# A conv-and-mixer kernel on one core: the second chunk's k, the inverse-transform constant and two pieces of w_mod asked for earlier

## The chip, the core and the metric

One core of a Trainium2 chip runs the whole kernel. The metric is device time in microseconds (us). The engines are TensorE (PE; PEld is its weight load), VectorE (DVE), ScalarE (ACT), GpSimd (POOL) and SyncE (SP). Each runs its own instructions strictly in the order in which they were written; this kernel's order is written out by hand, and no scheduler moves it. Loads are asked for by a queue, nearly all of them by SP's, a few at the start by ACT's. They are then carried by 16 shared DMA engines.

## What is computed

The reference takes a sequence of S = 2048 rows and D = 640 columns through two residual blocks, both modulated by a vector `c`:

```python
mod = (_silu(c) @ w_mod)                # 6 rows of 640: sa, ca, ga, sb, cb, gb
h = layernorm(x) * (1 + ca) + sa
k_shift[t] = sum_{s<4} k[t - s] * shift_k[:, s]          # short causal convolution
kv = k_shift * v
y = causal_conv(kv, ssm_k) + kv * ssm_D                  # 2048 taps, by FFT
x = x + ga * (h * y)
h = layernorm(x) * (1 + cb) + sb
x = x + gb * (gelu(h^T @ w1 + b1) @ w2 + b2)^T           # mixing over the 2048 rows
```

Here x is first `A_q`. All is float32.

## The kernel before

The first block runs over five chunks of 128 columns (`c` = 0 to 4). The causal convolution is done as a Fourier transform in two steps, both as matmuls with constants. `step1` (L211) is the first step: side 1 for the long taps `ssm_k`, side 0 for kv. Its four parts each end in an ACT copy to the tile `z` (L221). `f2` (L224) is the second step, in eight groups: 32 matmuls (64 records in the trace) against the constant `w2`, an ACT copy to `kt` (L238), two DVE products into `p` (`mul`, L57) and two POOL sums into `y` (`add`, L57). `i2` (L255) and `i1` (L274) go back; `gate` multiplies with the normalised q and adds to x.

Most elementwise work goes through the helper `TT` at L57, so these instructions are told apart by their tiles.

Before a chunk's transform, `kv_ops` (L172) works out kv in four groups, each with eight instructions: four products with taps, three sums, one product with v. DVE does groups 0, 2 and 3; POOL does group 1. The tile `in` (`T_in`) holds `KX`, the chunk's k, and behind it `VX`, its v. The tile `aux` holds the raw long taps (`KSR`) in its first half and, for the first chunk, kv (`X0`) in its second.

The start of the kernel is one long piece of hand-set order (L441 to L531), then the loop over chunks. What matters here:

- SP asks for chunk 0's k, v and taps, then the shift taps of chunk 1 (`load_taps(1)`, L482), the first half of the constant `w2` (`w2_load(0)`, L492), chunk 1's first k and v, its second k, the second half of `w2`, and its second v. Chunk 1's k goes over chunk 0's in the same tile `in`, so each half waits for DVE and POOL to have read the old one.
- The constant lands in the tile `xa`. ACT spreads it over `w0` and `w1` in eight instructions (`w2_part`, L476). The four of `w0` stand in ACT's order between the four copies of `step1(0, t)`; the four of `w1` stand between the copies of the first four groups of `f2`.
- Next SP asks for q, 32 loads of 160 KB each: rows 8 to 15 ("upper", tile `xb`) with the shift taps of chunk 2 and four small loads of biases and `c` between them (L523 to L528), then rows 0 to 7 (tile `xa`).
- Behind all of q come five pieces of w_mod (`mod_load`, L335; 960 KB each), and between the third and the fourth the constant `c_v1` of the back transform (1 MB). Then the long taps of chunk 1 and the k and v of chunk 2.
- In chunk 0, after `f2`, DVE takes the statistics of q's 16 row groups (L576, L577), then `rstd` (L323). ACT normalises 16 pieces into `aux` (`run(ac)`, L290). PE multiplies each w_mod piece by silu(c) (`mod_part`, L339). Behind the normalisation in ACT's order stands `mod_sum` (L346), which needs all five pieces. `mod_row` (L350) then spreads the result over all partitions, and only behind that in PE's order stands `i1` of chunk 0.

Places where the five pieces land before: two in `aux`, two in `in`, one in `p`.

Of the kernel before, what the change touches and what calls it, by code (L numbers as in the profile page):

```python
# [47 lines left out]
def mixer_kernel(ctx: ExitStack, tc: tile.TileContext, q, k, v, shift_k, ssm_k, ssm_D, w1, b1, w2, b2, c,  # L48
# [36 lines left out]
    KX = T_in[:, 0:2240].rearrange("p (n i) -> p n i", i=64)  # L85
    VX = T_in[:, 2240:4288].rearrange("p (n i) -> p n i", i=64)
    KSP = P.rearrange("p (i m) -> p i m", i=32)
    KSR, X0 = T_aux[:, 0:2048], T_aux[:, 2048:4096]
    A1 = T_aux[:, 2048:4096].rearrange("p (j d) -> p j d", j=16)
    KT = [T_kt[:, 512 * i:512 * i + 512] for i in range(2)]  # L90
    TV = T_kt[:, 1024:1536].rearrange("p (n i) -> p n i", i=64)
# [31 lines left out]
    TAP = tap[:, 512:768].rearrange("p (s i) -> p s i", s=4)  # L123


    def load_k(c, g, engs=(sync, sync), n=1):
        for h in range(2):
            r = slice(64 * h, 64 * h + 64)
            engs[h].dma_start(KX[r, 3 + 8 * g:3 + 8 * (g + n)],
                           dram(k, 8 * g * D + DC * c + 64 * h, [[32 * D, 64], [D, 8 * n], [1, 64]]))  # L130

    def load_v(c, g, engs=(sync, sync), n=1):
# [4 lines left out]

    def load_halo(c):
        for h in range(2):
            sync.dma_start(KX[64 * h + 1:64 * h + 64, 0:3],  # L140
                           dram(k, 29 * D + DC * c + 64 * h, [[32 * D, 63], [D, 3], [1, 64]]))

    def load_taps(c, eng=sync):
# [6 lines left out]

    def load_ks(c, upper=sync):
        for h in range(2):
            (sync, upper)[h].dma_start(KSR[64 * h:64 * h + 64].rearrange("p (i n) -> p i n", i=64),
                           dram(ssm_k, (DC * c + 64 * h) * S, [[32, 64], [S, 64], [1, 32]]))


    def perm_add(c, eng=pool):
        for h in range(2):
            r = KSR[64 * h:64 * h + 1].rearrange("p (i n) -> p i n", i=64)[:, :, 0]
            TT(eng, r, r, DR[64 * h:64 * h + 1], ALU.add)  # L160

    def perm(c):
        for i in (slice(0, 16), slice(16, 32)):
            act.activation(KSP.rearrange("p i (n e) -> p i e n", e=2)[:, i],  # L164
                           KSR.rearrange("p (i e n) -> p i e n", e=2, i=32)[:, i], AF.Copy)


    def taps():

        act.activation(TAP, TR.rearrange("p (i s) -> p s i", s=4), AF.Copy)  # L170

    def kv_ops(g, eng=dve, x=X):  # L172
# [4 lines left out]
        kx = lambda s: KX[:, 8 * g + 3 - s:8 * g + 11 - s, :]  # L177
# [267 lines left out]
    dve.memset(epsc, EPS)  # L445
    for h in range(2):
        dve.memset(KX[64 * h:64 * h + 1, 0:3, :], 0.0)
    both = (sync, act)
    load_taps(0, act)
    load_halo(0)  # L450
# [51 lines left out]
    run(kv_ops(1, pool))  # L502
# [7 lines left out]
    run(kv_ops(0))  # L510
    run(kv_ops(2))

    def load_q(js):

# [5 lines left out]
    pl = [three(t) for t in (T_aux, T_aux[:, 2048:3968], T_in[:, 192:2112], T_in[:, 2112:4032], P)]  # L520

    load_q(range(8, 12))
    load_taps(2)  # L523
    load_q(range(12, 14))
    sync.dma_start(stg[14:30, :], dram(b2, 0, [[128, 16], [1, 128]]))
    sync.dma_start(stg[30:35, :], dram(c, 0, [[128, 5], [1, 128]]))
    sync.dma_start(stg[0:13, :], dram(b1, 0, [[128, 13], [1, 128]]))
    sync.dma_start(stg[13:14, :].rearrange("p (h m) -> p h m", h=2), dram(b1, 1664, [[64, 1], [0, 2], [1, 64]]))  # L528
    load_q(range(14, 16))

    fill = kv_ops(3)  # L531

    def dv(n):
        for _ in range(min(n, len(fill))):
# [3 lines left out]
    for c in range(NC):  # L538
# [3 lines left out]
        for g in range(8):  # L542
            m_, a_ = f2(g)
            if pend_m:
                pend_m()
            if pend_a:
                pend_a()
            pend_a, pend_m = (pend_m and pa_next), m_
            pa_next = a_
            if c:  # L550
                for f_ in ac[2 * g:2 * g + 2]:
                    f_()
            elif g < 3:
                for i in ((0, 1), (2,), (3,))[g]:
                    w2_part(1, i % 2, 32 * (i // 2), 32)
                if g == 2:
                    load_q(range(8))
                    for kk in range(2):
                        mod_load(0, kk, (T_aux[:, 0:1920], T_aux[:, 2048:3968])[kk])
            if cn is None and g < 4:  # L560

                act.activation(X[:, 512 * g:512 * g + 1], epsc, AF.Copy)
                for b in range(2):
                    sync.dma_start(X[64 * b:64 * b + 64, 512 * g:512 * g + 512],
                                   dram(w1, (16 * b + g) * F, [[32 * F, 64], [1, 512]]))
            dv(-(-len(fill) // max((6 if c else 8) - g, 1)))
            if c and cn is not None and g == 3:
                perm_add(cn)
# [12 lines left out]
                load_taps(c + 3)  # L581
        if c == 0:
            for kk in range(2, 5):
                if kk == 3:
                    sync.dma_start(T_v1[:, 0:2048], c_v1)
                mod_load(0, kk, (T_in[:, 192:2112], T_in[:, 2112:4032], P[:, 0:1920])[kk - 2])
# [24 lines left out]
            load_v(2, 2, n=2)  # L611
            mod_sum(tap, T_kt[:, 0:640])
            pool.tensor_scalar(PW, TR.rearrange("p (i s) -> p s i", s=4), 1.0, None, op0=ALU.mult)
# [560 lines left out]
```

## Time and profile before

| | |
|---|---|
| times of three runs | 688.35, 692.94, 1027.85 us (median 692.94) |
| profiled execution: its own time | 682.19 us |
| profiled execution: its span | 680.1 us |
| PE busy | 624.6 us, 92% of the span |
| DVE busy | 499.0 us, 73% |
| ACT busy | 299.9 us, 44% |
| POOL busy | 129.5 us, 19% |
| moved by DMA | 81.23 MB, mean 119 GB/s |
| TensorE clock granted, mean | 0.985 of full |

The change touches the first 105 us of the span, some 15% of it. There DMA moves from 164 to over 400 GB/s. The later part, the mixer, is matmul work that the change leaves alone, so shares over the whole span say little; the prediction reads the first stages by themselves.

How such lines are read: in the timeline each row is the start, the busy time, the engine, the line, the operation, what it writes and reads, and in brackets the idle time of that engine before it with what ended the wait. `SPq` and `ACTq` are the sequencers that issue DMAs. The chain of waits is followed back from the last instruction: its rows are start, length and what the time went to; a DMA in it runs from its issue to its landing. A row by stretches has the stretch and its length, each engine's busy time, the granted clock, the busy share of the DMA engines (packets overlap, so it can pass 1) and the GB/s moved.

### The profile page before, as it was taken

To read this page: it belongs to the slowest core of one execution; us is meant where nothing else is said; L and a number is where in the kernel's file an instruction comes from. 1 tells how busy PE (TensorE), PEld (TensorE's weight loads), DVE (VectorE), ACT (ScalarE), POOL (GpSimd) and SP (SyncE) were. 2 spreads that over 40 slices of the span, in tenths; PEclk is the share of its full clock that TensorE was granted. 3 is DMA by queue.
4 is the path that set the end of the run, shared out by engine and by line. 5 is a ranking of instruction groups with operands and counts; after the bars stand their busy time and mean duration, and the time that the engine had idled before them with its cause. 6 is when DMAs were issued, how large, how long until landed. Compare 5 with 4: busy or idle time off the path is not lost.

```text
span 680.1 us, 20719 instructions
## 1 busy us (share of the span) xinstructions
PE 624.6 (92%) x9113; PEld 592.2 (87%) x9113; DVE 499.0 (73%) x867; ACT 299.9 (44%) x478; POOL 129.5 (19%) x149
## 2 busy tenths in 40 slices
PE   5889578989999999788899999999999989999997
PEld 2888277989989887688899889999999989999997
DVE  6799589979799279888866622321689779888996
ACT  1744645646547365547654222322344133333331
POOL 5562058226035142000000000000000520000000
PEclk9989889999999999999899999999999999999999
DMA  9978998365425343430308333334441634356601
GB/s 185 251 176 245 326 172 177 86 126 131 69 66 180 73 121 115 104 84 1 63 4 151 63 63 63 63 67 112 132 125 56 198 115 124 107 162 167 184 33 39
DMA packets 165522, 81.23 MB, mean 119 GB/s; under 512 B 90774, under 2 KB 157112, under 8 KB 165048
## 3 DMA queue, kind: packets, MB, share of 16 engines
q1 hardware_dynamic: 158516, 78.60, 47.0%
q10 hardware_dynamic: 6916, 1.31, 1.1%
q8 instruction: 71, 1.16, 0.7%
q14 instruction: 19, 0.16, 0.1%
HBM read 69.40 MB, written 10.49 MB: 117 GB/s over the span
## 4 chain that ended last, share of the span: by engine, by line
PE 63%; DVE 19%; DMA 7%; ACT 5%; issue 4%; POOL 1%; SPq 1%; DVEq 0%; ACTq 0%; POOLq 0%
PE pst L437 20%; PE pst L1033 17%; PE pst L1110 7%; PE pst L219 5%; PE pst L263 5%; PE pst L234 4%; DVE p L57 4%; PE pst L283 3%; DMA p<-in_w_mod_dram 2%; DVE tap L57 2%; DVE kt L57 2%; DVE sm L576 1%; PE pst L906 1%; DMA in<-in_A_v_dram 1%; ACT z L272 1%
## 5 line engine op out<-in xcount | busy, mean ns | idle before, releaser
L234 PE MATMUL pst<-z,w 128*64 128x64 f32 x2560 | 79.4, 225 | 13.3 <-DVE p L57 6.5
L234 PEld LDWEIGHTS pst<-z,w 128*64 128x64 f32 x2560 | 77.6, 140 | 15.6 <-issue 7.9
L221 ACT ACTIVATE z<-pst 128x1024 f32<-128x1024 f32 x40 | 42.9, 1073 | 42.1 <-PE pst L219 42.0
L57 POOL TENSOR_TENSOR y<-p 128x256 f32<-128x256 f32 x72 | 51.3, 743 | 41.2 <-DVE p L57 41.1
L57 DVE TENSOR_TENSOR p<-pst,kt 128x512 f32<-128x512 f32 x80 | 50.7, 682 | 6.0 <-ACT kt L238 6.0
L1033 PE MATMUL pst<-r_z,m_w 128*128 128x320 f32 x222 | 42.0, 312 | 2.2 <-DVE m_w L57 2.2
L869 ACT ACTIVATE pst<-pst,sm 128x640 f32<-128x640 f32 x13 | 10.0, 767 | 76.0 <-PE pst L437 76.0
L263 PEld LDWEIGHTS pst<-v,y 32*128 32x128 f32 x1280 | 38.5, 187 | 3.5 <-issue 3.0
L238 ACT ACTIVATE kt<-pst 128x512 f32<-128x512 f32 x40 | 23.9, 597 | 39.8 <-PE pst L234 24.1
L263 PE MATMUL pst<-v,y 32*128 32x64 f32 x1280 | 40.5, 272 | 0.4 <-issue 0.2
L219 PEld LDWEIGHTS pst<-v,p 128*64 128x64 f32 x640 | 34.8, 137 | 6.1 <-ACT p L164 2.9
L1021 ACT ACTIVATE m_w<-m_v 128x896 fp32r<-128x896 f32 x24 | 22.7, 951 | 36.9 <-PE pst L1033 16.8
L219 PE MATMUL pst<-v,p 128*64 128x128 f32 x640 | 36.7, 274 | 2.0 <-ACT p L164 2.0
L1033 PEld LDWEIGHTS pst<-r_z,m_w 128*128 128x128 f32 x222 | 35.2, 190 | 2.4 <-DVE m_w L57 2.4
L57 DVE TENSOR_TENSOR tap<-tap,kt 128x512 f32<-128x512 f32 x51 | 35.5, 697 | 1.3
L57 DVE TENSOR_TENSOR kt<-in,tap 128x512 f32<-128x512 f32 x51 | 35.0, 685 | 1.4
L57 POOL TENSOR_TENSOR m_p<-u_i,r_z 128x320 f32<-128x320 f32 x1 | 0.9, 881 | 183.4 <-issue 183.4
L219 PE MATMUL pst<-v,x 128*64 128x128 f32 x512 | 31.1, 275 | 2.2 <-DVE x L57 1.0
L219 PEld LDWEIGHTS pst<-v,x 128*64 128x64 f32 x512 | 27.9, 137 | 3.2 <-issue 1.6
L272 ACT ACTIVATE z<-pst 128x512 f32<-128x512 f32 x38 | 20.9, 645 | 21.1 <-PE pst L263 21.1
L283 PE MATMUL pst<-z,v 64*64 64x64 f32 x1280 | 23.9, 225 | 6.4 <-issue 3.7
L57 DVE TENSOR_TENSOR m_w<-m_v,m_w 128x896 fp32r<-128x896 f32 x24 | 27.9, 1166 | 2.3 <-ACT m_w L1021 1.8
(296 smaller groups left out, 1486.6 us busy)
## 6 DMA issues: line engine op xcount, KB each, us to landing
x<-in_B_w_dram SPq DMA_DIRECT2D x20, 512.0 KB
aux<-in_A_ssm_k_dram SPq DMA_DIRECT2D x9, 512.0 KB
m_x<-xs SPq DMA_DIRECT2D x28, 160.0 KB
out_dram<-m_x SPq DMA_DIRECT2D x28, 160.0 KB
m_v<-in_B_w_dram SPq DMA_DIRECT2D x9, 448.0 KB
in<-in_w_mod_dram SPq DMA_DIRECT2D x4, 960.0 KB
x<-in_B_w_dram SPq DMA_DIRECT2D x7, 448.0 KB
in<-in_A_v_dram SPq DMA_DIRECT2D x22, 128.0 KB
```

Source lines behind the costliest of these rows:

```text
L57: TT = lambda eng, o, a, b, op: eng.tensor_tensor(o, a, b, op=op)
L219: pe.matmul(ps[64 * ri:64 * ri + 64, o:o + 255:2], lhs, F1[:, 128 * ri:128 * ri + 128], start=True, stop=True)
L221: evac = lambda: act.activation(Z[:, side, t], ps.rearrange("p (a k e) -> p a k e", a=4, e=2), AF.Copy)
L234: pe.matmul(ps[64 * h:64 * h + 64, o:o + 64], W2[k1 // 32][:, 2 * (k1 % 32) + ri], rhs, start=True, stop=True)
L238: act.activation(kt.rearrange("p (m i) -> p m i", i=32), pv[:, :, 1], AF.Copy)
L263: pe.matmul(pp[qd // 2][:, o:o + 64], Y[p, ri, i:i + 2].rearrange("p i k -> p (i k)"), V2[p, 64 * ri:64 * ri + 64], start=ri == 0, stop=ri ...
L272: act.activation(o, i, AF.Copy)
L283: pe.matmul(ps[64 * b:64 * b + 64, 512 * e + 64 * jj:512 * e + 64 * jj + 64], V1[p, ri, n2], T2[p, :, 32 * ri + n2], start=ri == 0, stop=r ...
L437: pe.matmul(ps[0:m, h, 0:320], w_.bitcast(F32R), r_[:, 320 * h:320 * h + 320].bitcast(F32R), start=first and i == 0, stop=last and i == 2)
L1021: act.activation(W[n][0].bitcast(F32R), A[p, w_], AF.Copy)
L1033: pe.matmul(bank[n], w[:, i].bitcast(F32R), r.bitcast(F32R), start=i == 0 and k == 0, stop=i == 6 and k == 2)
L1110: pe.matmul(acc[s][:, h, 0:320], w[:, f_].bitcast(F32R), u[r + h].bitcast(F32R), start=f_ == 0 and k == 0, stop=f_ == NF - 1 and k == 2)
```

## The change

Four things are done together.

1. Chunk 1's k gets a home of its own, `KX1`, in the first 2240 columns of `aux`. For that, the long taps of chunk 0 and its kv (`X0`) move to the tile `y`. All of chunk 1's k (two halo loads and four of 256 KB) is asked for right behind chunk 0's last v, ahead of the shift taps and of `w2`.
2. `c_v1` and the first two pieces of w_mod are asked for between q's upper rows. The five pieces have new homes: `v`, `in`, `aux`, `in`, `p`. The long taps of chunk 1, which go over the third piece, are asked for behind `mod_part` of that piece and no longer behind the first.
3. The shift taps of chunk 2 and the four small loads are issued by POOL's queue, which stand in POOL's order behind chunk 1's kv and ahead of the sums of `f2`. No DMA was issued by POOL before.
4. Three more matmuls (ten for seven) at the start, whose output nobody reads, and two more short memsets for the new home.

```diff
-    KSR, X0 = T_aux[:, 0:2048], T_aux[:, 2048:4096]
+    KSR, X0 = T_aux[:, 0:2048], T_y[:, 0:2048]
+    KX1 = T_aux[:, 0:2240].rearrange("p (n i) -> p n i", i=64)
...
+    kx_of = lambda c: KX1 if c == 1 else KX
+    ksr_of = lambda c: T_y[:, 2048:4096] if c == 0 else KSR
...
+    load_halo(1)
+    load_k(1, 0, n=2)
+    load_k(1, 2, n=2)
     all_taps()
     load_taps(1)
     ps = psum()
-    for _ in range(7):
+    for _ in range(10):
...
     w2_load(0)
-    load_halo(1)
-    load_k(1, 0, n=2)
     load_v(1, 0, n=2)
     run(kv_ops(3, x=X0))
-    load_k(1, 2, n=2)
     w2_load(1)
     load_v(1, 2, n=2)
...
+    homes = [T_v1[:, 2048:3968], T_in[:, 192:2112], T_aux[:, 0:1920], T_in[:, 2240:4160], P[:, 0:1920]]
...
     load_q(range(8, 12))
-    load_taps(2)
+    load_taps(2, pool)
+    for o, t in ((30, dram(c, 0, [[128, 5], [1, 128]])), (14, dram(b2, 0, [[128, 16], [1, 128]])),
+                 (0, dram(b1, 0, [[128, 13], [1, 128]]))):
+        pool.dma_start(stg[o:o + t.shape[0], :], t)
+    pool.dma_start(stg[13:14, :].rearrange("p (h m) -> p h m", h=2), dram(b1, 1664, [[64, 1], [0, 2], [1, 64]]))
+    sync.dma_start(T_v1[:, 0:2048], c_v1)
     load_q(range(12, 14))
...
+    mod_load(0, 0, homes[0])
     load_q(range(14, 16))
-
-    fill = kv_ops(3)
+    mod_load(0, 1, homes[1])
+
+    fill = kv_ops(3, kx_=KX1)
...
             for kk in range(4):
                 mod_part(tap, kk, pl[kk])
-                if kk == 0:
+                if kk == 2:
                     load_D(1)
                     load_ks(1)
```

On SP's queue, from chunk 0's last v to chunk 1's last v, this is the order before (`in` holds k and v, `rows` the shift taps, `xa` the constant `w2`):

```order
L135 DMA in<-in_A_v_dram 64x8x64 x4
L145 DMA rows<-in_A_shift_k_dram 64x256 x2
L473 DMA xa<-in_const_w_dram 128x2048
L140 DMA in<-in_A_k_dram 63x3x64 x2
L129 DMA in<-in_A_k_dram 64x16x64 x2
L135 DMA in<-in_A_v_dram 64x16x64 x2
L129 DMA in<-in_A_k_dram 64x16x64 x2
L473 DMA xa<-in_const_w_dram 128x2048
L135 DMA in<-in_A_v_dram 64x16x64 x2
```

And now:

```order
L139 DMA in<-in_A_v_dram 64x8x64 x4
L144 DMA aux<-in_A_k_dram 63x3x64 x2
L133 DMA aux<-in_A_k_dram 64x16x64 x4
L149 DMA rows<-in_A_shift_k_dram 64x256 x2
L478 DMA xa<-in_const_w_dram 128x2048
L139 DMA in<-in_A_v_dram 64x16x64 x2
L478 DMA xa<-in_const_w_dram 128x2048
L139 DMA in<-in_A_v_dram 64x16x64 x2
```

All of k moved ahead of the shift taps and of both halves of `w2`; what stands ahead of the last v is the same set of loads in both.

Further down SP's queue, from q's upper rows (`xb`) to the last piece of w_mod, before (`g` holds the biases and `c`):

```order
L517 DMA xb<-in_A_q_dram 64x640 x8
L145 DMA rows<-in_A_shift_k_dram 64x256 x2
L517 DMA xb<-in_A_q_dram 64x640 x4
L525 DMA g<-in_B_b_dram 16x128
L526 DMA g<-in_c_dram 5x128
L527 DMA g<-in_B_b_dram 13x128
L528 DMA g<-in_B_b_dram 1x2x64
L517 DMA xb<-in_A_q_dram 64x640 x4
L517 DMA xa<-in_A_q_dram 64x640 x16
L336 DMA aux<-in_w_mod_dram 128x3x640 x2
L336 DMA in<-in_w_mod_dram 128x3x640
L585 DMA v<-in_const_v_dram 128x2048
```

And now:

```order
L522 DMA xb<-in_A_q_dram 64x640 x8
L534 DMA v<-in_const_v_dram 128x2048
L522 DMA xb<-in_A_q_dram 64x640 x4
L340 DMA v<-in_w_mod_dram 128x3x640
L522 DMA xb<-in_A_q_dram 64x640 x4
L340 DMA in<-in_w_mod_dram 128x3x640
L522 DMA xa<-in_A_q_dram 64x640 x16
L340 DMA aux<-in_w_mod_dram 128x3x640
L340 DMA in<-in_w_mod_dram 128x3x640
L340 DMA p<-in_w_mod_dram 128x3x640
```

Three large loads moved from behind q into its upper half, and six small ones left this queue.

They now stand in POOL's order, between the last instruction of chunk 1's kv (`x`) and the sums of `f2` (`y`):

```order
L57 TENSOR_TENSOR x<-t,in 128x8x32x2
L149 DMA rows<-in_A_shift_k_dram 64x256 x2
L532 DMA g<-in_c_dram 5x128
L532 DMA g<-in_B_b_dram 16x128
L532 DMA g<-in_B_b_dram 13x128
L533 DMA g<-in_B_b_dram 1x2x64
L57 TENSOR_TENSOR y<-p 128x8x32 x16
```

Before, the sums stood right behind that instruction.

ACT's order is the same as before. Its part that waits for `w2` reads, in the new kernel (`w_74` is `w0`, `w_75` is `w1`):

```order
L481 ACTIVATE w_74<-xa,v 128x32x32
L225 ACTIVATE z<-pst_262 128x4x128x2
L481 ACTIVATE w_74<-xa,v 128x32x32
L225 ACTIVATE z<-pst_281 128x4x128x2
L481 ACTIVATE w_74<-xa,v 128x32x32
L225 ACTIVATE z<-pst_300 128x4x128x2
L481 ACTIVATE w_74<-xa,v 128x32x32
L225 ACTIVATE z<-pst_319 128x4x128x2
L242 ACTIVATE kt<-pst_378 128x512
L481 ACTIVATE w_75<-xa,v 128x32x32 x2
L242 ACTIVATE kt<-pst_415 128x512
```

Nothing moved here; each copy to `z` and `kt` stands behind a piece of `w2`.

More of the change, by code (lines that the diff above doesn't have):

```diff
@@ L128, in load_k @@
             r = slice(64 * h, 64 * h + 64)
-            engs[h].dma_start(KX[r, 3 + 8 * g:3 + 8 * (g + n)],
+            engs[h].dma_start(kx_of(c)[r, 3 + 8 * g:3 + 8 * (g + n)],
                            dram(k, 8 * g * D + DC * c + 64 * h, [[32 * D, 64], [D, 8 * n], [1, 64]]))
@@ L139, in load_halo @@
         for h in range(2):
-            sync.dma_start(KX[64 * h + 1:64 * h + 64, 0:3],
+            sync.dma_start(kx_of(c)[64 * h + 1:64 * h + 64, 0:3],
                            dram(k, 29 * D + DC * c + 64 * h, [[32 * D, 63], [D, 3], [1, 64]]))
@@ L152, in load_ks @@
         for h in range(2):
[L153 removed]
+            (sync, upper)[h].dma_start(ksr_of(c)[64 * h:64 * h + 64].rearrange("p (i n) -> p i n", i=64),
                            dram(ssm_k, (DC * c + 64 * h) * S, [[32, 64], [S, 64], [1, 32]]))
@@ L158, in perm_add @@
         for h in range(2):
-            r = KSR[64 * h:64 * h + 1].rearrange("p (i n) -> p i n", i=64)[:, :, 0]
+            r = ksr_of(c)[64 * h:64 * h + 1].rearrange("p (i n) -> p i n", i=64)[:, :, 0]
             TT(eng, r, r, DR[64 * h:64 * h + 1], ALU.add)
@@ L164, in perm, with kv_ops @@
             act.activation(KSP.rearrange("p i (n e) -> p i e n", e=2)[:, i],
-                           KSR.rearrange("p (i e n) -> p i e n", e=2, i=32)[:, i], AF.Copy)
+                           ksr_of(c).rearrange("p (i e n) -> p i e n", e=2, i=32)[:, i], AF.Copy)
     def taps():
         act.activation(TAP, TR.rearrange("p (i s) -> p s i", s=4), AF.Copy)
-    def kv_ops(g, eng=dve, x=X):
+    def kv_ops(g, eng=dve, x=X, kx_=KX):
         S_, T_, W_ = (SV, TV, TAP) if eng is dve else (PS_.rearrange("p (n i) -> p n i", i=64),
@@ L176, in kv_ops @@
         w = lambda s: W_[:, None, s, :].to_broadcast([128, 8, 64])
-        kx = lambda s: KX[:, 8 * g + 3 - s:8 * g + 11 - s, :]
+        kx = lambda s: kx_[:, 8 * g + 3 - s:8 * g + 11 - s, :]
         ops = [lambda: TT(eng, S_, kx(3), w(3), ALU.mult)]
@@ L447, in mixer_kernel @@
         dve.memset(KX[64 * h:64 * h + 1, 0:3, :], 0.0)
+        dve.memset(KX1[64 * h:64 * h + 1, 0:3, :], 0.0)
     both = (sync, act)
@@ L501, in mixer_kernel @@
     all_taps()
-    run(kv_ops(1, pool))
+    run(kv_ops(1, pool, kx_=KX1))
     for t in range(4):
@@ L509, in mixer_kernel @@
             w2_part(0, (1, 0, 1)[t], 32 * (t > 0), 32)
-    run(kv_ops(0))
-    run(kv_ops(2))
+    run(kv_ops(0, kx_=KX1))
+    run(kv_ops(2, kx_=KX1))
     def load_q(js):
@@ L519, in mixer_kernel @@
     three = lambda t: [t[:, 640 * j:640 * j + 640] for j in range(3)]
-    pl = [three(t) for t in (T_aux, T_aux[:, 2048:3968], T_in[:, 192:2112], T_in[:, 2112:4032], P)]
+    homes = [T_v1[:, 2048:3968], T_in[:, 192:2112], T_aux[:, 0:1920], T_in[:, 2240:4160], P[:, 0:1920]]
+    pl = [three(t) for t in homes]
     load_q(range(8, 12))
-    load_taps(2)
+    load_taps(2, pool)
[4 more added lines that the diff above has]
+    sync.dma_start(T_v1[:, 0:2048], c_v1)
     load_q(range(12, 14))
[L525 to L528, printed above, removed]
+    mod_load(0, 0, homes[0])
     load_q(range(14, 16))
-    fill = kv_ops(3)
+    mod_load(0, 1, homes[1])
+    fill = kv_ops(3, kx_=KX1)
     def dv(n):
@@ L557, in mixer_kernel @@
                     load_q(range(8))
-                    for kk in range(2):
-                        mod_load(0, kk, (T_aux[:, 0:1920], T_aux[:, 2048:3968])[kk])
             if cn is None and g < 4:
@@ L583, in mixer_kernel @@
             for kk in range(2, 5):
-                if kk == 3:
-                    sync.dma_start(T_v1[:, 0:2048], c_v1)
-                mod_load(0, kk, (T_in[:, 192:2112], T_in[:, 2112:4032], P[:, 0:1920])[kk - 2])
+                mod_load(0, kk, homes[kk])
             step1(0, 0)
```

## The prediction

> **What bounds the kernel now.** I read the chain of waits for the first 105 us first, since the change reaches no further. These are its parts where something other than steady work was waited for:
>
> ```profile
> 0.71 2.61 DMA rows<-in_A_shift_k_dram
> ...
> 20.57 7.03 DMA in<-in_A_k_dram
> ...
> 31.20 8.10 DMA in<-in_A_v_dram
> ...
> 42.60 3.56 PE pst L234 x64
> ...
> 67.05 15.83 DMA p<-in_w_mod_dram
> 82.88 0.04 issue
> 82.92 1.54 PE tap L343 x12
> 84.46 0.02 issue
> 84.48 0.71 ACT kt L347
> ```
>
> Two waits at the start, for chunk 1's k (until 27.59) and its second v (until 39.30), then a long one for the last w_mod piece, until 82.88. Behind it come `mod_sum` at 84.48, the `mod_row`s and `i1`. Next, how busy the DMA engines were while that w_mod piece waited its turn:
>
> ```profile
> 20.00:24.00 4.00, 4.00 (x79) 4.00 (x74) 3.79 (x7) 2.33 (x3) 1.88 (x2) 1.00 0.96 307
> 24.00:32.00 8.00, 7.49 (x134) 7.03 (x130) 5.38 (x8) 7.31 (x8) 4.08 (x4) 1.00 1.19 217
> 42.00:62.00 20.00, 18.44 (x509) 17.98 (x509) 19.49 (x41) 8.24 (x12) 11.39 (x16) 0.91 0.67 194
> 72.00:76.00 4.00, 2.19 (x23) 1.01 (x24) 1.29 (x5) 2.30 (x6) 1.37 (x2) 1.00 1.03 421
> 76.00:80.00 4.00, 0.43 (x6) 0.00 (x0) 2.43 (x2) 4.00 (x11) 0.00 (x0) 1.00 1.03 400
> ```
>
> The last two columns are the share and the GB/s. With `w2` at 20 to 24 us, and with k and v at 24 to 32, the engines are full, at 307 and 217 GB/s. While q is asked for, at 42 to 62, they are at 0.67 and 194 GB/s; with w_mod alone they reach 400 to 421. So between 42 and 62 DMA could have moved some 20 x (410 - 194) = 4.3 MB more: SP, with one 160 KB piece at a time, doesn't ask fast enough. Last the rows of the engines:
>
> ```profile
> 25.28 1.13 ACT L476 ACTIVATE w<-xa,v 128x1024 f32<-128x1024 f32 x1
> 28.77 1.08 ACT L221 ACTIVATE z<-pst 128x1024 f32<-128x1024 f32 x1
> 32.80 1.02 ACT L221 ACTIVATE z<-pst 128x1024 f32<-128x1024 f32 x1
> 33.88 5.82 PE L234 MATMUL pst<-z,w 128*64 128x64 f32 x192 [1.90 <-ACT z L221]
> 36.01 0.60 ACT L238 ACTIVATE kt<-pst 128x512 f32<-128x512 f32 x1 [2.18 <-PE pst L234]
> 36.50 2.18 ACT L476 ACTIVATE w<-xa,v 128x1024 f32<-128x1024 f32 x2
> 38.58 0.59 ACT L238 ACTIVATE kt<-pst 128x512 f32<-128x512 f32 x1
> 39.85 0.69 DVE L57 TENSOR_TENSOR x<-tap,in 128x512 f32<-128x512 f32 x1 [1.14 <-DMA in<-in_A_v_dram]
> 41.18 1.28 DVE L57 TENSOR_TENSOR p<-pst,kt 128x512 f32<-128x512 f32 x2
> 42.97 1.28 DVE L57 TENSOR_TENSOR p<-pst,kt 128x512 f32<-128x512 f32 x2
> 54.41 1.29 DVE L57 TENSOR_TENSOR p<-pst,kt 128x512 f32<-128x512 f32 x2
> ```
>
> `f2` starts at 33.88, but DVE comes to its first product (`mul` of group 0) only at 41.18, behind the kv that waited for v. Its input `kt` was ready at 36.61, so this stage has 4.57 us of slack on ACT and PE. From the second `mul` (42.97) to the eighth (54.41) it is 11.44 us for six groups, 1.9 each. Then DVE takes q's statistics without a break, and this follows:
>
> ```profile
> 68.34 1.97 PE L219 MATMUL pst<-v,x 128*64 128x128 f32 x32
> 70.23 1.28 PE L343 MATMUL tap<-aux,sm 128*32 128x320 f32 x12
> 74.74 3.18 ACT L290 ACTIVATE aux<-xa,sm 128x128 f32<-128x128 f32 x8 [1.69 <-POOL t L613]
> 77.83 3.17 ACT L290 ACTIVATE aux<-xb,sm 128x128 f32<-128x128 f32 x8
> 84.48 0.70 ACT L347 ACTIVATE kt<-tap 96x640 f32<-96x640 f32 x1 [3.48 <-PE tap L343]
> ```
>
> ACT ends the normalisation at 81.00 and idles 3.48 us for w_mod. That is what the second part of the change can win, and no more: with w_mod in time, ACT's own work ends last there.
>
> **The change part by part.**
>
> *w_mod and `c_v1` earlier.* Behind q's last load stood 5 x 0.98 + 1.05 = 5.96 MB, landed at 82.88. Now 3.02 MB of it goes into q's stretch, where 4.3 MB had room; at 410 GB/s that takes 7.4 us off the tail. SP's queue gets no longer: three issues in, six out,
>
> ```profile
> 41.77 1.18 SPq L145 DMA_DIRECT2D rows<-in_A_shift_k_dram  x2
> 63.04 2.08 SPq L336 DMA_DIRECT2D aux<-in_w_mod_dram  x2
> 67.05 1.44 SPq L336 DMA_DIRECT2D p<-in_w_mod_dram  x1
> ```
>
> and the third to fifth piece wait, as before, for chunk 1's kv and the sums from `p`; these end 1.43 behind the eighth `mul`, so by 60 even if that comes late, and SP is then still with q. So the last piece lands at about 82.88 - 7.4 = 75.5. PE is through `step1(0, 3)` at 70.31 and needs five `mod_part`s of 1.3 to 1.5, so 77; ACT is later, at 81.0. `mod_sum` moves from 84.48 to 81.05: **-3.4 us**, if nothing ahead moves. The long taps of chunk 1, now behind `mod_part` 2, go two parts later on PE, at about 74, but onto a queue that is nearly empty; `perm(1)` needs them behind `mod_row`, as before. Nothing.
>
> *k ahead of `w2`.* DMA is full here, so order is all that changes. Before, k's first half landed at 27.59 behind taps, `w2`(0) and halo. Now the same loads and k's second half (0.52 MB, 2.4 us at 217 GB/s) precede the end of `w2`(0): it lands at **30.0**. Before, ACT used it at 25.28 without a wait. For the last v nothing changes, the same bytes stand ahead of it: 39.30 again, and `mul` of group 0 can't start before 41.18. The wait for k on DVE (27.71) turns into one for the shift taps, which now land at about 27.59 + 2.4 less `w2`(0), 1.05 MB or 3.4 us at 307 GB/s, = 26.6; with 0.6 for the taps DVE is ready at 27.3. The v then holds it anyway. Gain there: nothing.
>
> The loss: from 30.0 ACT has four pieces of `w0` and four copies to `z`, with no gaps, 4 x 1.13 + 4 x 1.08 = 8.84, so `f2` starts at 38.9 in place of 33.88. That is 5.0 late against 4.57 of slack. PE meanwhile does three of four `step1` parts; the fourth needs the buffer that the first copy frees at 32.2, and takes 1.97. PE is idle from 34.2 to 38.9. Before, an idle time of 2.91 us on PE was followed by this:
>
> ```profile
> 39.00:42.50 3.50, 0.69 (x24) 0.55 (x20) 2.62 (x5) 1.20 (x2) 0.56 (x1) 0.99 0.68 190
> 42.50:46.00 3.50, 3.40 (x66) 3.42 (x68) 3.50 (x7) 1.63 (x2) 2.77 (x5) 0.52 0.71 200
> ```
>
> The granted clock fell to 0.52, and the group begun at 42.60 took 3.56 us, not 5.82 / 3 = 1.94. I take it that group 0 now runs so: it ends at 42.5, `kt` is there at 43.1, `mul` 0 at 43.2. Then ACT has two pieces of `w1` (2.18) before the next copy (0.59), so `mul` 1 is at 46.0, where it was 42.97: 3.05 late. Six groups at 1.87 (PE's 5.82 / 3 less overlap, and DVE's 1.28 + 0.69 of kv less overlap) end at 57.2 against 54.41: **+2.8 us**. The statistics, `rstd` and the normalisation all follow behind and move by it.
>
> [...]
>
> *Six loads on POOL.* No row shows a DMA issued by POOL. Before, POOL ended kv and began the sums here:
>
> ```profile
> 37.15 1.30 POOL L57 TENSOR_TENSOR x<-t,in 128x512 f32<-128x512 f32 x1
> 41.94 1.43 POOL L57 TENSOR_TENSOR y<-p 128x256 f32<-128x256 f32 x2 [3.49 <-DVE p L57]
> ```
>
> It starts this kv as before (its taps land at 26.6, a product takes 1.3), so it is free at 38.45 again. `mul` 2, now at 47.9, needs the first sums (1.43) done, so POOL has until 46.4: six loads in 8.0 us, 1.33 each, cost nothing. The ends for the unknown price: SP's issue of the same shift taps, 1.18 for two, 0.59 each; and the 2.61 us from issue to landing in the chain's first row, if POOL stayed with each until it landed. I take the low end: an issue doesn't wait for its landing on SP. Nothing, hidden by the wait for `mul` 0.
>
> *The rest.* Three more dummy matmuls delay `step1(1, 0)` by half a microsecond, ahead of ACT's wait for `w2`; nothing. Two memsets on one row, before the first load lands: nothing.
>
> **Sum.** -3.4 + 2.8 = **-0.6 us** against the profiled execution (682.19 us, span 680.1), so 681.6. The runs shown are above it: 688.35 and 692.94, and one of 1027.85 that I leave out; 692.94 is the median. I put the forecast at the middle one of the three that agree, 688.35: 688.35 - 0.6 = **687.7 us**.
>
> **The rivals.**
>
> *PE keeps its clock, or `w2` lands sooner* (faster). With the clock full, group 0 ends at 40.8, `mul` 0 is at 41.5, `mul` 1 at 44.2: 1.2 late, the eighth 1.0, net -2.4. With `w2` in time the whole 3.4 is won. 684.9 to 686. For it: the idle time before was 2.9 us at another point, and the clock row is the only case. Against: DMA was full at 24 to 32, so the bytes must come out somewhere.
>
> *POOL is held by its loads* (slower). At 2.61 each it is free at 38.45 + 15.7 = 54.1, 7.7 behind 46.4; each sum and `mul` behind moves by as much: -0.6 + 7.7 = +7.1, 695.4. It decides from 1.33 us a load upward. For it: nothing on POOL shows a price. Against: SP's 0.59. [...]
>
> *w_mod lands no earlier* (no change). If q and w_mod share what q got alone, the last piece lands at 82.9 again; ACT's end at 81.0 + 2.8 = 83.8 hides behind it, and the sum is zero: 688.35. Against it stand the 400 to 421 GB/s.
>
> **How the numbers follow.** The forecast 0.45, the faster rival 0.25, POOL 0.15, no earlier w_mod 0.15. All four lie within 1.1% of the median, and a measurement of this kernel tells 2% from no change, not less. What could show over 2% is the spread of the runs themselves: from 682.2 to 692.9 is 1.6%. So faster by over 2% 0.06, within 2% 0.89, slower 0.05. The range goes from the lowest level with the faster rival, 682.2 - 3.4 = 678.8, to POOL's 695.4: 679 to 696.
>
> **What would show it.** Right: ACT waits some 4 us for `xa` at 26 to 30; `f2` starts near 38.9; the granted clock falls there; DMA above 300 GB/s from 42 to 62; ACT's `kt` at L347's successor comes right behind the sixteenth normalisation, near 83.9; POOL's loads end before `mul` 0. Wrong: `f2` starting near 34, or w_mod still waited for by PE behind the normalisation, or DVE's products waiting for POOL.

## The result, and the profile after

The changed kernel takes 694.91 us (median of 20 runs, 689.64 to 699.85), the kernel before 688.34 (20 runs): the ratio is 1.0101, with a 95% interval of 1.0074 to 1.0127. It is 1% slower, some 7 us. The forecast was 0.6 us faster. It lies within 2% as forecast, but on the other side, and not by any of the rivals. That 694.91 still falls into the stated range of 679 to 696 is luck: the upper end was POOL's price, which was not paid.

The profiled execution took 694.99 us with a span of 693.2, close to its median; that of the kernel before had been 6 us ahead of its own (682.19). The chain of waits of the changed kernel, its parts from the copy of `w2` to `mod_sum`:

```profile
24.50 5.72 DMA xa<-in_const_w_dram
30.24 1.15 ACT w L481
...
38.28 11.34 PE pst L238 x328
49.62 3.30 issue
52.91 5.21 PE pst L238 x127
58.12 3.93 issue
62.05 2.96 PE pst L238 x57
...
87.74 3.94 ACT aux L294 x10
91.68 0.59 ACT kt L351
```

The reader should see two things. The long wait for w_mod, which stood here before the change (15.83 us, to 82.88), is gone, and `mod_sum` comes right behind ACT's last normalisation. But w_mod is not earlier. The weight load for its fifth piece still waits for the landing, until 85.55, where the forecast had 75.5:

```profile
85.55 0.69 PEld L347 LDWEIGHTS tap<-p,sm 128*32 128x32 f32 x12 [0.63 <-DMA p<-in_w_mod_dram]
```

The wait left the chain only because everything else is later still. And in its place PE stands still twice inside the first `f2`, for 3.30 and 3.93 us, on "issue": time in which it waits for no semaphore that the profile knows. Nothing in the prediction has a name for this. VectorE's products show what it costs; the first, the fifth, the sixth and the eighth:

```profile
42.35 1.29 DVE L57 TENSOR_TENSOR p<-pst,kt 128x512 f32<-128x512 f32 x2 [0.42 <-ACT kt L242]
...
50.31 1.27 DVE L57 TENSOR_TENSOR p<-pst,kt 128x512 f32<-128x512 f32 x2
56.83 1.29 DVE L57 TENSOR_TENSOR p<-pst,kt 128x512 f32<-128x512 f32 x2 [4.65 <-ACT kt L242]
...
65.80 1.29 DVE L57 TENSOR_TENSOR p<-pst,kt 128x512 f32<-128x512 f32 x2 [5.22 <-ACT kt L242]
```

Against before (41.18 and 54.41) the first product is 1.2 late and the eighth 11.4. ACT is named in the brackets, but ACT itself waited for PE. Statistics, normalisation and `mod_sum` (91.59, before 84.48) all move behind it, `mod_sum` by 7.1 us, about what the medians differ by. The same stretches as in the prediction, of the kernel after, with two short ones behind the idle times:

```profile
42.00:62.00 20.00, 12.83 (x385) 12.55 (x383) 12.89 (x21) 7.84 (x11) 9.99 (x14) 0.91 1.04 260
54.00:62.00 8.00, 4.12 (x113) 3.98 (x109) 3.75 (x6) 1.20 (x2) 2.83 (x4) 0.89 1.06 228
76.00:80.00 4.00, 4.00 (x128) 3.93 (x126) 3.86 (x13) 1.24 (x3) 0.00 (x0) 1.00 1.02 394
52.40:55.60 3.20, 2.69 (x50) 2.69 (x52) 0.00 (x0) 0.00 (x0) 0.07 (x1) 0.50 1.07 249
62.60:65.90 3.30, 3.30 (x59) 3.30 (x55) 0.10 (x1) 0.60 (x1) 0.00 (x0) 0.50 0.76 166
```

From 42 to 62 DMA is now full (share 1.04), yet it moves 260 GB/s and from 54 on only 228, not the 400 that w_mod reaches when alone (394 at 76 to 80). And behind each idle time the granted clock is 0.50.

What PE waits for can be seen in the queues of DMA. These are the queue rows of three neighbouring windows, 50.0 to 51.6, 51.6 to 59.3 and 59.3 to 61.0; the columns are packets, MB and share:

```profile
q1 hardware_dynamic: 179, 0.44, 97.8%
q8 instruction: 1, 0.02, 5.0%
...
q1 hardware_dynamic: 814, 1.87, 106.2%
...
q1 hardware_dynamic: 187, 0.41, 99.1%
q8 instruction: 1, 0.02, 5.1%
```

One packet of q8, the queue of kind "instruction", shortly before PE goes on at 52.91, none for nearly 8 us, and the next shortly before it goes on at 62.05. By the trace they end at 51.53 and 60.75, 1.4 and 1.3 us before PE goes on. It is the same in all thirteen profiles: each of PE's 40 idle times on issue between 34 and 112 us ends 1.3 to 1.6 us behind the end of a q8 packet. Over the whole span the page counts 71 such packets with 1.16 MB, 16 KB each, and 9119 rows of PE and 9119 of its weight loads; 18238 / 71 is 257. So a packet is put at the next 257 or so of PE's instructions, an estimate from these counts; between the two idle times PE executed 127 products and 127 weight loads, 254 rows: about one packet.

Last, SP's own waits from 40 to 75 us, whose loads for q come behind the early ones:

```profile
SPq L522 <- DMA in<-in_w_mod_dram: 4.1, 1, 4.1
SPq L522 <- DMA v<-in_w_mod_dram: 3.7, 1, 3.7
SPq L522 <- DMA v<-in_const_v_dram: 3.3, 1, 3.3
```

SP waited three times for one of the early loads to land before it issued more of q: 11.1 us. Its last issue of q ended at 73.2, before the change at 63.0. Before the change none of its waits in 40 to 70 was for a landing.

### The profile page after: what moved, and what is told of

The parts are those of the page before. It is cut to its first block, busy times and chain, and to the rows that moved or that the text cites. A ratio compares the mean times of both kernels' runs of the same rounds, so it can differ in the third digit from the quotient of the medians.

```text
span 693.2 us, 20744 instructions
## 1 busy us (share of the span) xinstructions
PE 634.6 (92%) x9119; PEld 601.0 (87%) x9119; DVE 499.6 (72%) x869; ACT 299.4 (43%) x478; POOL 134.8 (19%) x155
## 3 DMA queue, kind: packets, MB, share of 16 engines
q8 instruction: 71, 1.16, 0.7%
## 4 chain that ended last, share of the span: by engine, by line
PE 67%; DVE 15%; ACT 7%; issue 5%; DMA 3%; SPq 1%; POOL 1%; ACTq 0%; DVEq 0%; POOLq 0%
PE pst L441 20%; PE pst L1038 17%; PE pst L1115 7%; PE pst L238 6%; PE pst L223 6%; PE pst L267 6%; PE pst L287 3%; DVE p L57 2%; DVE tap L57 2%; ACT z L276 2%; DVE kt L57 1%; PE pst L911 1%; PE tap L347 1%; ACT z L225 1%; DVE sm L546 1%
## 5 line engine op out<-in xcount | busy, mean ns | idle before, releaser
L238 PE MATMUL pst<-z,w 128*64 128x64 f32 x2560 | 82.0, 228 | 18.7 <-issue 7.7
L238 PEld LDWEIGHTS pst<-z,w 128*64 128x64 f32 x2560 | 80.1, 143 | 21.1 <-issue 12.7
L287 PEld LDWEIGHTS pst<-z,v 64*64 64x64 f32 x1280 | 24.8, 156 | 10.8 <-issue 6.7
L287 PE MATMUL pst<-z,v 64*64 64x64 f32 x1280 | 26.9, 243 | 7.4 <-issue 4.7
L57 DVE TENSOR_TENSOR kt<-in,tap 128x512 f32<-128x512 f32 x42 | 28.8, 685 | 1.2
```

The lines of the kernel that those rows point to most:

```text
L57: TT = lambda eng, o, a, b, op: eng.tensor_tensor(o, a, b, op=op)
L238: pe.matmul(ps[64 * h:64 * h + 64, o:o + 64], W2[k1 // 32][:, 2 * (k1 % 32) + ri], rhs, start=True, stop=True)
L287: pe.matmul(ps[64 * b:64 * b + 64, 512 * e + 64 * jj:512 * e + 64 * jj + 64], V1[p, ri, n2], T2[p, :, 32 * ri + n2], start=ri == 0, stop=r ...
```

## The experiments

The theory, **instructions**: PE runs out of program, because the packet with its next 257 or so instructions comes late when DMA is full. With it goes a second, **half the partitions**: q's stretch had little room, since loads to 64 partitions move at little more than half the rate (with DMA full 228 GB/s from 54 to 62, where w_mod to 128 moved 394). Rivals: **late w2** (the order of k and `w2`, with the half clock behind it, does it all), **a wait of the program** that the profile doesn't show, and **the rest** of the change (homes, POOL's loads). Ratios are to the kernel before, with 95% intervals; "idle" is PE's idle time on issue in the first `f2`, "eighth" the start of the eighth product, in the profiled execution.

| kernel | ratio | idle, us | eighth |
|---|---|---|---|
| the change | 1.0101 (1.0074 to 1.0127) | 3.30, 3.93 | 65.80 |
| loads behind q | 0.9991 (0.9961 to 1.0020) | 0.16, 0.35 | 59.27 |
| w2 first | 1.0011 (0.9982 to 1.0040) | 0.86, 4.46 | 62.77 |
| both back | 0.9966 (0.9943 to 0.9990) | 0.41, 0.35 | 54.00 |

**c_v1 and w_mod behind q again**, all else as in the change:

```diff
-    sync.dma_start(T_v1[:, 0:2048], c_v1)
...
-    mod_load(0, 0, homes[0])
...
-    mod_load(0, 1, homes[1])
...
                     load_q(range(8))
+                    for kk in (0, 1,):
+                        mod_load(0, kk, homes[kk])
...
             for kk in range(2, 5):
+                if kk == 3:
+                    sync.dma_start(T_v1[:, 0:2048], c_v1)
                 mod_load(0, kk, homes[kk])
```

> c_v1 and the first two pieces of w_mod go back behind q; everything else is the changed kernel. Theory 'instructions' (PE's two idle times of 3.30 and 3.93 us in the first f2, put down to issue, are waits for the next block of its instructions, whose transfer stands behind a backlog of loads): no such idle time is left in the first f2, the eighth product is near 57.2 in place of 65.8, and the time lies 2.8 us over the kernel before, near 691, some 4 us under the changed kernel. Rival 'late w2' (f2 starts 4.4 us late and the half clock that follows does the rest): idle times stay, eighth product still near 65, time 694 to 695 or more, since w_mod is late again.

The idle times are all but gone from `f2` (0.16 and 0.35 us), and the time is the kernel before's, 688.23 us, some 3 under what was expected for it. The eighth product came at 59.27, 2 later than expected. PE's timeline:

```profile
39.70 12.43 PE L238 MATMUL pst<-z,w 128*64 128x64 f32 x328 [2.25 <-ACT z L225]
52.29 3.94 PE L238 MATMUL pst<-z,w 128*64 128x64 f32 x127 [0.16 <-issue]
...
75.16 1.11 PE L267 MATMUL pst<-v,y 32*128 32x64 f32 x30 [2.26 <-issue]
```

The pieces of 328 and 127 are the same as in the change, so PE crosses the same places in its program here, only without a wait. The third row shows what had not been expected: w_mod, now loaded from 62 on, makes PE wait at later places of this kind, 1.04 us in `step1` at 68.01 and 2.26 in `i2`. The wait went where the full DMA went.

**w2 ahead of the second chunk's k again**, early c_v1 and w_mod kept:

```diff
-    load_halo(1)
-    load_k(1, 0, n=2)
-    load_k(1, 2, n=2)
     all_taps()
...
     w2_load(0)
+    load_halo(1)
+    load_k(1, 0, n=2)
     load_v(1, 0, n=2)
...
+    load_k(1, 2, n=2)
     w2_load(1)
```

> w2's first half goes back ahead of the second chunk's k and halo, as before; the early c_v1 and w_mod stay. Theory 'instructions': f2 starts near 33.9 again, but the idle times on issue stay, two of 3 to 4 us; some 2.8 us under the changed kernel, near 692. Rival 'late w2': the idle times go, eighth product near 54.4, and with w_mod early the time is some 3 us under the kernel before, near 685.

```profile
33.56 7.37 PE L238 MATMUL pst<-z,w 128*64 128x64 f32 x192 [2.09 <-ACT z L225]
...
50.22 3.94 PE L238 MATMUL pst<-z,w 128*64 128x64 f32 x127 [0.86 <-issue]
58.62 3.35 PE L238 MATMUL pst<-z,w 128*64 128x64 f32 x57 [4.46 <-issue]
```

`f2` starts at 33.56 again, and the second idle time stays and is longer. Late `w2` isn't its cause. The first one shrinks from 3.30 to 0.86, where 3 to 4 were expected, so the order of `w2` and k may have a part in that one. The time, 688.03 us, lay between the two forecasts of 692 and 685.

**Both undone** (the two edits together):

> Both moves of loads undone. What stays of the change: the homes in memory, the small loads on POOL, three more dummy products. If the order of loads is the whole cause, under either theory: within 1.5 us of the kernel before, 687 to 690, eighth product near 54.4. Rival 'the rest' (homes or POOL's loads cost it): 693 or more.

Ratio 0.9966, 684.29 us, below the 687 to 690 expected: faster than the kernel before by 0.1 to 0.6%. So the loss lies in the order of the loads, and the rest of the change is a small gain. Against this run `w2` late alone costs 0.25%, the early loads alone 0.45%, both 1.35% (each ratio is known to about 0.3%). By the eighth product the parts come to 5.3 and 8.8 us, and both to 11.8, less than their sum. Whether the two make each other worse stays open.

**The same program, shifted.** 32 products of two columns behind the dummy products, 64 more rows of PE ahead of `f2`:

```diff
+    for _ in range(32):
+        pe.matmul(ps[:, 0:2], T_in[:, 192:320], T_in[:, 192:194], start=True, stop=True)
```

> The changed kernel with 32 products of two columns behind the dummy products, while PE has nothing to do: 64 records of PE more ahead of the first f2, half of the 128 that lie between the two idle times. Theory 'instructions': the idle times on issue move by 64 records, the first behind 264 or 392 records of f2 in place of 328, the second again some 128 further; the time is that of the changed kernel within 1 per cent. Rival 'a wait of the program' (data, a buffer, a semaphore that the profile does not show): the idle times stay at 328 and 455 records.

```profile
15.75 10.86 PE L495 MATMUL pst<-in 128*128 128x2 f32 x64
...
45.70 5.78 PE L238 MATMUL pst<-z,w 128*64 128x64 f32 x137 [2.10 <-ACT z L225]
53.52 3.95 PE L238 MATMUL pst<-z,w 128*64 128x64 f32 x127 [2.04 <-issue]
61.65 9.67 PE L238 MATMUL pst<-z,w 128*64 128x64 f32 x248 [4.17 <-issue]
```

PE now stops behind 137 and 264 rows of `f2`. That is 328 - 64 = 264, as expected, and one packet (127) earlier, 137, which was not foreseen. In the other runs with idle times in this stage they stand behind 201, 328 or 455 rows of `f2`, again 127 apart. The idle times sit at fixed distances in PE's stream of instructions and not at a place of the computation, which settles **instructions** against **a wait of the program**. The time missed what was expected: ratio 1.0232 (1.0207 to 1.0257), 1.3% over the change. The first row shows a reason: the small products were not cheap, 10.86 us for 64 rows, at a granted clock of 0.64 on average, and `f2` began at 45.70, 7.4 later than in the change.

**q to all partitions at once.** In the changed kernel, one load to 128 partitions for each pair of loads to 64; q's rows then land in other partitions than the computation wants, so it computes with permuted rows:

```diff
-            for b in range(2):
-                sync.dma_start(XH[j // 8][64 * b:64 * b + 64, j % 8], dram(q, (16 * b + j) * D, [[32 * D, 64], [1, D]]))
+            sync.dma_start(XH[j // 8][:, j % 8], dram(q, j * D, [[16 * D, 128], [1, D]]))
```

> The changed kernel, but each row of q's layout is loaded by one transfer to all 128 partitions in place of two to 64 each; the rows of q land in other partitions than the computation wants, the bytes are the same. Theory 'half the partitions' (a transfer to 64 partitions moves at half the rate once DMA is full, so the stretch of q's upper rows was nearly full before the change, at 225 GB/s and not at 410): packets of 2560 bytes stay near 0.11 us, DMA moves 350 GB/s or more from 42 to 58, q is issued by 60 in place of 73, and the time falls by 5 us or more against the changed kernel, to 690 or less. Rival 'mixing' (w_mod beside q slows both, whatever the partitions): rate stays near 230 GB/s, q's last issue at 70 or later, time near 695. Under 'instructions' PE may still idle on issue once or twice before 58, as long as DMA is full, and not behind it.

**Two rows of q in each load to 64 partitions**: as few issues as there, but half the partitions:

```diff
-        for j in js:
+        for j in js[::2]:
             for b in range(2):
-                sync.dma_start(XH[j // 8][64 * b:64 * b + 64, j % 8], dram(q, (16 * b + j) * D, [[32 * D, 64], [1, D]]))
+                sync.dma_start(XH[j // 8][64 * b:64 * b + 64, j % 8:j % 8 + 2],
+                               dram(q, (16 * b + j) * D, [[32 * D, 64], [D, 2], [1, D]]))
```

> The changed kernel, with two of q's rows in each transfer to 64 partitions: half as many issues on SP, as in the run with all partitions, but half of the partitions at a time. Theory 'half the partitions': rate stays near 230 GB/s from 54 on, PE idles on issue as in the changed kernel or longer (twice the bytes stand in each slot ahead of a block of instructions), time 693 to 700. Rival 'issues' (SP's 32 issues held q up, not the rate): q is issued by 60, time 690 or less.

By stretches, with all partitions:

```profile
48.00:62.00 14.00, 10.67 (x292) 10.40 (x294) 8.14 (x14) 2.39 (x4) 6.62 (x10) 0.87 1.04 395
```

and with two rows to 64 partitions:

```profile
54.00:68.00 14.00, 9.86 (x244) 9.41 (x238) 6.82 (x12) 2.40 (x4) 4.96 (x8) 0.88 1.04 245
```

At the same share of 1.04 the same engines move 395 GB/s of q and w_mod to all partitions, and 245 with q to 64. **Half the partitions** is shown: w_mod is mixed in and SP has 16 issues in both, so neither is the cause. Two other stretches with q to 64 partitions come close to the 245: 228 in the changed kernel from 54 to 62, with w_mod among it, and 225 before the change in the same stretch, with q alone, at a share of 0.78.

The times: 1.0077 (1.0050 to 1.0103) with all partitions, 692.68 us, where 690 or less was expected; and 1.0275 (1.0230 to 1.0319), 705.15, with two rows, above the expected range. SP was through with q at 57.5, as expected, but PE still stood idle while DMA was full, at 395 GB/s too. All partitions:

```profile
48.10 5.44 PE L238 MATMUL pst<-z,w 128*64 128x64 f32 x127 [2.38 <-issue]
54.50 3.94 PE L238 MATMUL pst<-z,w 128*64 128x64 f32 x127 [0.96 <-issue]
60.71 2.60 PE L238 MATMUL pst<-z,w 128*64 128x64 f32 x57 [2.27 <-issue]
```

Two rows:

```profile
49.28 5.50 PE L238 MATMUL pst<-z,w 128*64 128x64 f32 x127 [2.25 <-issue]
56.72 5.49 PE L238 MATMUL pst<-z,w 128*64 128x64 f32 x127 [1.94 <-issue]
64.42 1.90 PE L238 MATMUL pst<-z,w 128*64 128x64 f32 x57 [2.21 <-issue]
```

From one start to the next PE gets a packet every 6.2 to 6.4 us here, every 7.4 to 7.7 us there, and after 9.1 in the changed kernel; it can use one up in 3.94. With both moves undone the distance is 4.3:

```profile
47.02 3.94 PE L238 MATMUL pst<-z,w 128*64 128x64 f32 x127 [0.41 <-issue]
51.31 1.90 PE L238 MATMUL pst<-z,w 128*64 128x64 f32 x57 [0.35 <-issue]
```

So even with room this stage is at the edge: there it was 0.35 to 0.41 us short at each packet. In the runs below with the small loads on SP and with c_v1 last, and in both profiles of the kernel before, `f2` has no such idle time; in the two profiles of before the granted clock was 0.86 on average from 42 to 54, with both undone 1.00 from 42 to 62.

**c_v1 alone early** (both undone, but c_v1 at its place in the change):

> w2 first, the two pieces of w_mod behind q, and only c_v1 (1.05 MB) early: a third of the bytes. Theory 'backlog' (what stands ahead of a block of instructions sets the wait): at most one idle time on issue in f2, under 2 us, and w_mod is in 2.6 us earlier than with all three behind q; the time is that of the run with both moves undone or up to 2 us less, 682.5 to 685. Rival 'any large load in q's stretch costs as much': 686 to 688.

**The same in four pieces**, one ahead of each of q's rows 12 to 15:

```diff
-    sync.dma_start(T_v1[:, 0:2048], c_v1)
-    load_q(range(12, 14))
-    load_q(range(14, 16))
+    for j in range(12, 16):
+        o = slice(512 * (j - 12), 512 * (j - 12) + 512)
+        sync.dma_start(T_v1[:, o], c_v1[:, o])
+        load_q((j,))
```

> As the run with c_v1 alone early (one idle time of 3.42 us on issue in f2), but c_v1 in four pieces of 0.26 MB, one ahead of each of q's rows 12 to 15. Theory 'backlog': no slot of SP holds 1 MB, fewer bytes stand ahead of a block of instructions at its request, and the idle time falls to 2 us or less; the time is 1 to 2 us under that run, ratio 0.994 to 0.996. Rival 'full is full': DMA is as busy over the same 10 us, the idle time stays at 3 us or splits into two, ratio 0.997.

Ratios 0.9969 (0.9938 to 0.9999) and 0.9971 (0.9938 to 1.0004): neither gains over both undone. In us they are 686.66 and 685.96; the first lies in its rival's 686 to 688 and not in the 682.5 to 685 of the theory, and the second ratio is the rival's 0.997. The idle time on issue was 3.42 us in one case, where under 2 was expected, and 2.48 in the other, expected at 2 or less; c_v1 whole, then in pieces:

```profile
49.62 7.21 PE L238 MATMUL pst<-z,w 128*64 128x64 f32 x184 [3.42 <-issue]
```

```profile
56.63 3.26 PE L238 MATMUL pst<-z,w 128*64 128x64 f32 x57 [2.48 <-issue]
```

One packet in place of two is late, but by 2.5 to 3.4 us. The traces show that a packet is not slow itself: in `f2` the ones that PE waited for took 1.0 to 1.6 us in every run. It starts late. From PE's going on to the start of the next one it is 1.2 to 1.5 us with both undone and with the loads behind q, and 3.7 to 6.5 in the change and the runs where DMA was full and a second idle time followed. Whether that goes by the bytes that stand ahead of the packet stays open: pieces shortened the wait by 0.94, but the packet hit was another one.

**Small loads on SP again**, with both moves undone:

```diff
-    load_taps(2, pool)
+    load_taps(2)
...
-        pool.dma_start(stg[o:o + t.shape[0], :], t)
...
+        sync.dma_start(stg[o:o + t.shape[0], :], t)
...
```

> Both moves of loads undone, and the small loads and the shift taps back on SP's queue: of the change only the homes and three dummy products stay. If the 2.3 us that the run with both moves undone was under the kernel before come from POOL's loads (SP saves 3.2 us of issues between q's rows): the time of the kernel before, ratio 1.000, 686 to 689. If they come from the homes or the dummy products: ratio 0.997 again, 684 to 686.

Ratio 0.9993 (0.9965 to 1.0022), the kernel before's time. It fits a gain from POOL's loads and none from the homes: SP is through with q at 63.99, with both undone at 61.14, and `mod_sum`, which waits for w_mod in both, starts at 87.24 and 83.08. But the interval overlaps that of both undone, so the gain isn't shown.

**c_v1 behind the last w_mod piece.** Nothing goes early; what isn't needed first goes last:

```diff
             for kk in range(2, 5):
-                if kk == 3:
-                    sync.dma_start(T_v1[:, 0:2048], c_v1)
                 mod_load(0, kk, homes[kk])
+            sync.dma_start(T_v1[:, 0:2048], c_v1)
```

> Both moves of loads undone, and c_v1 behind the fifth piece of w_mod in place of between the third and the fourth; nothing goes early. The last two pieces land 2.6 us sooner (1.05 MB at 400 GB/s) without one byte more in q's stretch, c_v1 lands near 80 and its three copies on VectorE (3.7 us) are done by 84. Theory 'what waits at the end is the order behind q': the sum of w_mod goes from 83.1 to 80.6, the first i1 from 87.1 to 84.6, PE idles on issue as little as in the run with both undone; 2 to 2.5 us under that run, ratio 0.993. Rival 'c_v1 is next': the copies end behind 85 and i1 stays at 87; ratio 0.9966 again.

Ratio 0.9953 (0.9919 to 0.9987): with both undone at 0.9966 the best, and faster than the kernel before; the two can't be told apart. w_mod is no longer what ends last: PE waits 0.67 us for its last piece at 78.58, and `mod_sum` follows the normalisation at once. But it didn't come to 80.6:

```profile
68.84 1.11 PE L267 MATMUL pst<-v,y 32*128 32x64 f32 x30 [1.15 <-issue]
69.88 3.43 PE L223 MATMUL pst<-v,x 128*64 128x128 f32 x32
```

```profile
80.70 3.17 ACT L294 ACTIVATE aux<-xb,sm 128x128 f32<-128x128 f32 x8
83.77 0.68 ACT L351 ACTIVATE kt<-tap 96x640 f32<-96x640 f32 x1
```

PE waited 1.15 us for a packet in `i2`, took 3.43 us in place of 1.97 for its next `step1` (granted clock 0.88 on average from 64 to 78), and ACT, which copies these out ahead of `rstd`, started the normalisation late. The same two costs, at another place. `i1` came at 87.80, as the rival had it, but it waited for ACT's `g` and not for the copies of c_v1.

**The kernel before, a second profile:**

> The kernel before, unchanged, for a second profile of it: its first one ended 6 us ahead of its median. If the stage ahead of the first i1 is steady, i1 starts within 1 us of 87.4 again and the 6 us lie in the later stages; if not, differences of profiles by a few us say nothing there either.

```profile
86.57 2.53 PE L354 MATMUL pst<-kt,sm 1*128 1x320 f32 x12 [0.81 <-ACT kt L347]
89.86 6.52 PE L283 MATMUL pst<-z,v 64*64 64x64 f32 x255 [0.76 <-ACT g L361]
```

`i1` starts at 89.86, 2.5 later than in the first profile, and not within 1: `mod_sum` was already 1.3 late (85.81 against 84.48), and `mod_row` took 2.53 here, at a granted clock of 0.50 (82 to 92), and 1.37 there, at 0.96 (85 to 87). Up to the eighth product the two stay within 1 us (`f2` at 34.81 and 33.88). So two profiles of one kernel differ by 2.5 us at `i1`. Behind it the thirteen profiles take from 592.4 to 597.6 us, in no order that follows the edits: of the 13.1 us between the first spans of the two kernels 8.2 stand at `i1` and 4.9 behind it, whose cause is open. So the table's ratios, not the spans, carry what is worth a few us.

## Why the prediction was wrong

*The step that failed* is "between 42 and 62 DMA could have moved some 20 x (410 - 194) = 4.3 MB more". It took the rate of w_mod, which goes to 128 partitions, for that of q, which goes to 64. Full, q's stretch moves 228 GB/s (54 to 62 after). In the profile of before, q alone moved as much in its second half, at a share of 0.78:

```profile
54.00:62.00 8.00, 7.42 (x189) 7.07 (x189) 7.80 (x22) 3.91 (x6) 2.15 (x4) 1.00 0.78 225
```

By that the q of before, at 194 GB/s, used 17 of the 20 us, and the other 3 at 400 GB/s are room for some 1.2 MB (an estimate from these rows), not 4.3. Measured, the 20 us took in 1.3 MB more (260 in place of 194 GB/s). The share of 0.67 alone was no measure of room. 3.02 MB went in, and the stretch ran full until 64.

*The term that came of it*: -3.4 us for w_mod. It needed the last piece at 75.5, and that piece kept PE waiting until 85.55, 2.7 later than before. That `mod_sum` is bound by ACT came out as forecast, but not for the forecast's reason. Alone, the early loads cost +0.45% in place of -0.5%, because a full DMA held up two things here that the prediction priced at nothing. "SP's queue gets no longer" was counted in issues (three in, six out), while SP waited 11.1 us for landings and came to its last three pieces of w_mod at 73 to 75 in place of 65 to 67. And PE waited 3.30 and 3.93 us for packets of q8, which the page counts among the work of the same 16 DMA engines; the chain of waits runs through this one, and what SP's waits cost by themselves isn't shown. The rows for this were in the profile of before: the queue q8 in its list of queues, and a row on issue in `i1`, 2.52 us. The prediction used neither.

What PE paid for a packet (71 of them, 16 KB each) went with the room on DMA: in `f2` it was no idle time, or 0.16 to 0.41 us, with room, and 0.86 to 4.46 us with DMA full.

*The term `w2` late, +2.8*, was of the right kind. `w2` came at 30.24 (forecast 30.0), `f2` at 38.28 (38.9), the first product at 42.35 (43.2). Up to the fifth product, ahead of the first idle time, the loss was 1.5 (50.31 against 48.81). Alone (loads behind q against both undone) it costs 5.3 us at the eighth product, nearly twice the term, and at the end 0.25% or 1.7 us, not clear of the noise.

*The half clock* was expected behind the idle time ahead of `f2`, and came there (0.71 on average from 34 to 42) as well as behind both new ones. The 127 products between them took 5.21 us in place of 3.94 and the 57 behind 2.96 in place of 1.90; the two idle times and these 2.3 us make 9.6 of the 11.4 by which the eighth product is late. That an idle time of 2.9 us brings the half clock is not certain: ahead of the same group PE stood idle 2.91 us before and 2.92 with both undone, and in the second case the clock stayed at 1.00 from 42 to 62.

*POOL's loads*, at nothing, were right: they held up no sum. Six loads took 3.4 us, and the first sum waits for VectorE's product, not for them:

```profile
38.64 1.30 POOL L149 DMA_DIRECT2D rows<-in_A_shift_k_dram  x2
...
41.48 0.51 POOL L533 DMA_DIRECT2D g<-in_B_b_dram  x1
43.13 1.44 POOL L57 TENSOR_TENSOR y<-p 128x256 f32<-128x256 f32 x2 [1.14 <-DVE p L57]
```

The 0.3% by which both undone beats the kernel before may be their gain on SP, which issues q without these six in between; the run with them back on SP fits that and doesn't show it.

*The rivals.* "w_mod lands no earlier" came nearest: from 54 on q and w_mod did share the rate of q alone (228 and 225 GB/s), and the last piece came in later than before. But it priced that at zero, since it looked at w_mod's landing alone and not at who else stands behind it. None of the four cases had a loss that comes from DMA being full, and so the sign was wrong.

## What to carry to other kernels

Room on DMA is the rate that these very loads reach when the engines are full, less the rate they move now; the busy share alone doesn't give it (0.67 from 42 to 62 before, and only 1.3 MB more once it was full). At the same share of 1.04, loads to 64 partitions with w_mod among them reached 245 GB/s here, loads to 128 reached 395. Before a stretch of dense small products is filled up with early loads, look for the instruction queue and for idle time on issue: `f2`, which got through 127 products and their weight loads in 3.94 us, paid for a full DMA directly (3.30 and 3.93 us) and again in clock (0.50 just behind each, 2.3 us). Where a late load is the wait, its order among the late ones comes first: c_v1 behind w_mod took that wait away without a byte in the early stretch, though the time didn't fall by an amount that can be told from both undone.

## What the runs showed of the hardware

The queue of kind "instruction" moved 71 packets of 16 KB, one to 257 of PE's products and weight loads, and the page counts them at 0.7% of the 16 DMA engines: with room on DMA, PE waited up to 0.41 us for a packet in `f2`; with DMA full, its idle times were 0.86 to 4.46. The packets that it waited for took 1.0 to 1.6 us each either way; they started 1.2 to 1.5 us behind PE's going on with room, and 3.7 to 6.5 with DMA full. Loads to 64 partitions, with w_mod among them, filled the engines at 228 to 245 GB/s, where loads to 128 reached 395. Products of two columns were not cheap: 64 rows, each with a weight load of 128 columns, took 10.86 us, 0.17 each at a granted clock of 0.64 on average.
